# Long-convolution kernels summed in four column tiles instead of two, with half-size staging, an earlier phase product and the first kernel in the scratch tile

## The chip, the cores and the metric

The program runs on one core of one Trainium2 chip. The core has a matrix engine (PE, with its weight loads shown apart as PEld), a vector engine (DVE), an engine for activations and copies (ACT), a general engine (POOL) and an engine that issues transfers (SP); each works through its own list of instructions in order and waits on semaphores for the others. Transfers are carried by sixteen DMA engines; here nearly all are issued by SP and POOL. The metric is the device time of one execution in microseconds (us), given as the median of the runs shown.

## The reference

Four layers on a sequence of 2048 positions with 640 channels: a state-space convolution, attention, the same convolution again, the same attention again, each on a layer norm of x and added to x. The convolution's kernel is computed from the parameters and is the same both times:

```
x = A_u
x = x + _A_ref(_layernorm(x), ...)      # long convolution, kernel K
x = x + _B_ref(_layernorm(x), ...)      # attention, 32 heads of 20, one key and value head
x = x + _A_ref(_layernorm(x), ...)
x = x + _B_ref(_layernorm(x), ...)

# inside _A_ref: D = 640 channels, N = 128 states, L = 2048
dt = exp(log_dt)[:, None];  A = A_re + 1j*A_im;  logdA = dt*A;  dB = dt*Bc
P = exp(logdA[:, :, None] * arange(L))
K = einsum("dn,dnl,dn->dl", Cc, P, dB).real
y = irfft(rfft(u padded to 2L) * rfft(K padded to 2L))[:L] + u * Dskip
```

So K takes 640 x 2048 sums over 128 complex states, before the first convolution can use its spectrum.

## The kernel before

The program has three kinds of stage, one after another: the kernels' generation (`_kgen`), two convolution layers (`conv_layer`, with the kernels' spectra in `kernel_spectra` ahead of the first), and two attention layers.

**Generation.** A position l is split as 32 i + j, with i in 0..63 and j in 0..31. The sum over the states then is a product of two small factors per channel: one of size 128 states x 64 (called `E1R`, for even terms, and `M1`, for odd ones) and one of 128 x 32 (`C2`, `S2`). Channels go in 20 units: unit u takes sixteen pairs of channels ("par" is 0 or 1 within a pair). Sixteen of the units have their pair 128 channels apart and belong to runs of eight that fill two blocks of 128 channels each (q is 0 and 1); the last four fill the fifth block (q is 2). For a unit the code has these steps:

- `phase(u, h)`: PE multiplies a small table into a PSUM tile `ph` (two matmuls of 512 columns), of which there is one; DVE rounds it (`r`) and subtracts (`f`). h is 0 and 1.
- `trig(u, h)`: ACT takes the absolute value (`fa`), a sine and a cosine (`s`, `c`). POOL sets one column of the first pair of tiles ahead of it.
- `sizes(u, k)`, `exps(u, k)`: PE makes exponents in a tile `pe` (two buffers), ACT takes their exponential (`m`), for k of 0, 1, 2.
- `products(u, k)`: DVE multiplies sizes and sines, two operations for each k: `e1r`, then `m`, then `c` and `s`.
- `sums(u, ds)`: PE forms the sums over the states into a tile `pk` (two buffers). For each of 16 values of d and for each of the two terms, two matmuls, one per par, stand in the two halves of the array's columns: 64 columns of weights (`e[u][:, d, par]`) and 32 moving columns (`c[u][:, d, par]`).
- `store(u)`: ACT copies `pk` into a staging tile `kst` for the whole q (one buffer). With the last unit of q, SP writes it to `kd` in DRAM: for q of 0 and 1 with rows of 8 KB, for q of 2 with runs of 256 bytes.

The three engines PE, ACT and DVE keep the order in which the code is written, which is a loop over u in which unit u's phase and sizes, unit u-1's products and unit u-2's sums are interleaved by hand. Within an iteration PE has: `sizes(u, 0)`, sums for d 0 to 2, `sizes(u, 1)`, sums for d 3 to 5, the product of `phase(u + 1, 0)`, sums 6 to 9, the product of `phase(u + 1, 1)`, and the rest (with `sizes(u, 2)` at one of two places as u is odd or even). DVE has: `products(u-1, 0)`, the two operations of `phase(u+1, 0)`, `products(u-1, 1)`, those of `phase(u+1, 1)`, `products(u-1, 2)`, and in iterations 5 to 12 statistics of x. With unit 20 (there is none) the tables are freed and POOL issues the load of the transform's weights `wf`, 4 MB.

**Spectra.** `kernel_spectra` loads the five blocks from `kd` through POOL's queue: four into one tile `kts`, the fifth into a tile `ktl`, which also takes the skip weights. Both lie where tiles of the generation lay. For each block DVE adds the skip weight to position 0 (`skip`, 128 elements), PE multiplies by `wf` (`raw`, four PSUM tiles `zk` of 32 passes each), ACT copies out (`Azk`), DVE forms a transform over eight (`radix`, `fft8`) with two helper tiles `B` and `R`, and SP writes the spectrum. PE and ACT are one block ahead of DVE.

Of the kernel before, what the change touches and what calls it, by code (L numbers as in the profile page):

```python
# [37 lines left out]
SAFE = ((LIMIT - 1e-6) / 1.002) ** 2  # L38

# [103 lines left out]
class Net:  # L143
# [152 lines left out]
    def _kgen(self, ctx):  # L296
# [39 lines left out]
        C1, S1, C2, S2, M1, M2, E1R, F, PE_, PK, KST = ({} for _ in range(11))  # L336
        KST[0] = bp.tile([P, 32, 128], F32, tag="kst", bufs=1, name="kst0")
# [14 lines left out]
        def phase(u, h):  # L352

            pp = kp.tile([P, 1024], F32, tag="ph", bufs=1, name=f"ph{u}{h}")
            src, col, rows = ((tb, 0, 48), (ta, 512, 96))[h]
            for par in range(2):
                nc.tensor.matmul(pp[:, 512 * par : 512 * par + 512], grp(src, u, par, rows),
                                 kg[0:rows, col : col + 512], start=True, stop=True)
            r = bp.tile([P, 1024], BF16, tag="r", bufs=2, name=f"r{u}{h}")
            self.magic_round(r, pp)  # L360
            F[u, h] = bp.tile([P, 1024], F32, tag="f", bufs=4, name=f"f{u}{h}")
            nc.vector.tensor_tensor(F[u, h], pp, r, ALU.subtract)
# [51 lines left out]
        def sums(u, ds):  # L414

            if u not in PK:
                PK[u] = kp.tile([P, 512], F32, tag="pk", bufs=2, name=f"pk{u}")
            for d in ds:
                for e, c, first in ((E1R, C2, True), (M1, S2, False)):
                    for par in range(2):  # L420
                        nc.tensor.matmul(PK[u][64 * par : 64 * par + 64, 32 * d : 32 * d + 32],  # L421
                                         e[u][:, d, par], c[u][:, d, par], start=first, stop=not first)

        def store(u):
            q, r, _, _, run = units[u]
            if r == 0 and q > 0:
                KST[q] = bp.tile([P, 32, run], F32, tag="kst", bufs=1, name=f"kst{q}")
            kst = KST[q]
            nc.scalar.activation(kst[:, :, 16 * r : 16 * r + 16],
                                 PK[u].rearrange("p (d j) -> p j d", d=16), AF.Copy)  # L430
            if 16 * (r + 1) == run:
                for par in range(2):
                    for jh in range(2):
                        src = kst[64 * par : 64 * par + 64, 16 * jh : 16 * jh + 16, :]
                        if run == 128:
                            dst = self.kd[2 * q + par, 64 * jh : 64 * jh + 64]
                            nc.sync.dma_start(dst, src.rearrange("p t d -> p (t d)"))
                        else:
                            dst = self.kd[4, 64 * jh : 64 * jh + 64].rearrange(
                                "p (t d) -> p t d", d=DC)[:, :, 64 * par : 64 * par + 64]  # L440
                            nc.sync.dma_start(dst, src)


# [4 lines left out]
        with tc.manual_schedule(engines=engines):  # L448
            for h in range(2):
                phase(0, h)  # L450
            for u in range(n + 3):
# [18 lines left out]
                if tot:  # L470
                    sums(u - 2, range(3, 6))
# [9 lines left out]
                if tot:  # L481
                    sums(u - 2, range(6, 10))
# [4 lines left out]
                if tot:  # L487
                    sums(u - 2, range(10, 13))
# [8 lines left out]
                if tot:  # L497
                    sums(u - 2, range(13, 16))
# [11 lines left out]
    def conv_setup(self, ctx):  # L510
        tc = self.tc
        if not self.wfs:
            self.conv_weights(self.nc.sync)
        self.cvp = ctx.enter_context(tc.tile_pool(name="cvp", bufs=1, reuse_waits="tile"))

        self.B = self.cvp.tile([P, 16, 256], F32, name="B")
        self.R = self.cvp.tile([P, 8, 256], F32, name="R")
# [166 lines left out]

    def kernel_spectra(self):

        nc, cv = self.nc, self.cvp

        kts = cv.tile([P, 4, 16, DC], F32, tag="wi", name="kts")
        ktl = cv.tile([P, 24, DC], F32, tag="xn", name="ktl")  # L690
        ks = [kts[:, c] for c in range(4)] + [ktl[:, 0:16]]
        dsk = ktl[0:1, 16:21]
        nc.gpsimd.dma_start(dsk.rearrange("p c d -> p (c d)"), self.ins["A_Dskip"][None, :])
        for c in range(NCH):
            nc.gpsimd.dma_start(ks[c].rearrange("p t d -> p (t d)"), self.kd[c])

        def skip(c):
            k = ks[c][0:1, 0]
            nc.vector.tensor_tensor(k, k, dsk[:, c], ALU.add)

        skip(0)
        Z = {0: self.raw(ks[0], "k0")}
        for c in range(NCH):
            if c + 1 < NCH:
                skip(c + 1)
                Z[c + 1] = self.raw(ks[c + 1], f"k{c + 1}")
            A = cv.tile([P, 16, 256], F32, tag="kh", bufs=2, name=f"kn{c}")
            weave(self.radix(Z.pop(c), A) + fft8(nc, A, self.B, self.R, -1), ())
            nc.sync.dma_start(self.kh[c], A.rearrange("p s d -> p (s d)"))

    def conv_layer(self, nm, first):
# [4 lines left out]
        B, R = self.B, self.R  # L716
        tt = nc.vector.tensor_tensor
        with tc.manual_schedule(engines={mybir.EngineType.PE, mybir.EngineType.Activation,
# [7 lines left out]
            if first:  # L726
                self.kernel_spectra()

# [604 lines left out]
```

## Time and profile before

| what | us |
|---|---|
| median of 3 runs (3068.69 to 3069.82) | 3069.56 |
| the profiled execution | 3071.17 |
| its span, from the first to the last instruction | 3069.4 |
| from the span's start to the first copy of sums into `kst` | 85.3 |
| from there to the last such copy | 252.7 |
| first matmul of the spectra | 344.1 |

The profile is of one execution. Its views name an instruction by engine, line of the code, operation and `out<-in`; "x4" after it is how many were put together in a row. In a timeline the columns are the start, the time that the row took, the engine, the line and the operation, and in square brackets how long the engine had stood idle before and what ended that. In a list of waits the numbers are the total, how often, and the longest. A single-precision matmul stands in the trace as two passes. Ends of matmuls are modelled, so the distance between starts says more than the duration. The line numbers are those of the kernel before; after the change they are higher.

### The profile page before, as it was taken

What the parts mean: (1) busy time and instruction counts of PE and PEld (TensorE: products, weight loads), DVE (VectorE), ACT (ScalarE), POOL (GpSimd) and SP (SyncE); (2) the same over time, 40 slices, a digit from 0 to 9 for tenths busy, and PEclk for the clock granted to TensorE, in tenths of its full rate; (3) what the DMA queues carried; (4) which work ended last, traced back from release to release, by engine and by line L of the source; (5) the groups of instructions that cost most, each with busy time, mean ns of one, the idle gap of its engine ahead of it and who ended that gap; (6) DMA issues with size and microseconds to landing.
All of it is one profiled execution on the core that took longest, in us unless ns stands there. A gap on an engine that the chain in (4) does not pass through costs nothing. (4 is left out here: it accounts for less than half of the span.)

```text
span 3069.4 us, 52317 instructions
## 1 busy us (share of the span) xinstructions
PE 2874.8 (94%) x21696; PEld 1362.8 (44%) x21696; DVE 1404.4 (46%) x1793; ACT 2428.3 (79%) x2910; POOL 41.5 (1%) x113
## 2 busy tenths in 40 slices
PE   2888898989899999999999989798999999999999
PEld 0555887867323323333233479673223333333233
DVE  7888799972122232232222399922122222222223
ACT  5777343353899999999999633446999999999997
POOL 0000000000100000000000000000000000000000
PEclk9999999989999999999999999899999999999999
DMA  6010551123300010000100210132000100100100
GB/s 143 18 29 17 177 220 56 38 83 131 112 24 25 22 28 22 24 25 22 27 23 24 112 55 28 50 125 79 23 22 25 39 27 24 39 25 21 45 19 22
DMA packets 72177, 158.82 MB, mean 52 GB/s; under 512 B 21509, under 2 KB 27653, under 8 KB 67797
## 3 DMA queue, kind: packets, MB, share of 16 engines
q1 hardware_dynamic: 65880, 137.70, 14.9%
q0 software_dynamic: 4080, 16.67, 1.5%
q8 instruction: 175, 2.87, 0.4%
q10 hardware_dynamic: 1968, 0.98, 0.1%
q14 instruction: 74, 0.60, 0.1%
HBM read 95.22 MB, written 48.04 MB: 47 GB/s over the span
## 5 line engine op out<-in xcount | busy, mean ns | idle before, releaser
L1134 ACT ACTIVATE pt<-scb 128x1024 f32<-128x1024 f32 x1024 | 942.2, 1115 | 7.5 <-PE scb L1130 5.8
L1134 ACT ACTIVATE pt<-scd 128x1024 f32<-128x1024 f32 x1024 | 942.2, 1118 | 7.0 <-PE scd L1130 5.5
L1144 PE MATMUL pod<-pt,vt 128*32 128x512 f32 x4096 | 546.9, 606 | 4.4 <-DVE on L1161 0.8
L1144 PE MATMUL pob<-pt,vt 128*32 128x512 f32 x4096 | 546.9, 606 | 4.3
L1130 PE MATMUL scb<-qpb,kt 62*128 62x512 f32 x2048 | 386.0, 451 | 6.2 <-PEq L1079 5.8
L1130 PE MATMUL scd<-qpd,kt 62*128 62x512 f32 x2048 | 385.8, 451 | 5.8 <-PEq L1079 5.5
L1130 PEld LDWEIGHTS scd<-qpd,kt 62*128 62x128 f32 x2048 | 166.1, 185 | 402.0 <-ACT pt L1134 392.3
L1130 PEld LDWEIGHTS scb<-qpb,kt 62*128 62x128 f32 x2048 | 165.9, 185 | 402.1 <-ACT pt L1134 392.6
L1192 DVE TENSOR_TENSOR x<-pyd,x 128x320 f32<-128x320 f32 x146 | 71.7, 491 | 561.0 <-PE pyd L1204 561.0
L1192 DVE TENSOR_TENSOR x<-pyb,x 128x320 f32<-128x320 f32 x146 | 71.7, 491 | 547.7 <-PE pyb L1204 547.7
L1164 DVE RECIPROCAL rc<-rc 128x512 f32<-128x512 f32 x62 | 207.9, 3353 | 2.1
L1144 PEld LDWEIGHTS pob<-pt,vt 128*32 128x32 f32 x4096 | 80.7, 108 | 178.3 <-issue 160.3
L1144 PEld LDWEIGHTS pod<-pt,vt 128*32 128x32 f32 x4096 | 80.6, 108 | 177.7 <-issue 159.7
L421 PE MATMUL pk<-s,m 128*64 128x32 f32 x1280 | 130.8, 295 | 13.3 <-DVE s L412 13.3
L421 PE MATMUL pk<-c,e1r 128*64 128x32 f32 x1280 | 132.1, 297 | 11.4 <-DVE c L411 11.2
L421 PEld LDWEIGHTS pk<-c,e1r 128*64 128x64 f32 x1280 | 105.3, 221 | 79.6 <-issue 52.2
L579 PE MATMUL za<-xna,wf 128*128 128x256 f32 x512 | 113.0, 383 | 2.7 <-ACT xna L733 2.7
L421 PEld LDWEIGHTS pk<-s,m 128*64 128x64 f32 x1280 | 108.1, 226 | 15.9 <-DVE s L412 15.9
L579 PE MATMUL zc<-xnc,wf 128*128 128x256 f32 x512 | 111.5, 379 | 2.7 <-ACT xnc L733 2.7
L581 ACT ACTIVATE Aa<-za 128x1024 f32<-128x1024 f32 x16 | 16.4, 1023 | 118.3 <-PE za L579 116.9
L581 ACT ACTIVATE Ac<-zc 128x1024 f32<-128x1024 f32 x16 | 16.4, 1024 | 113.7 <-PE zc L579 113.7
L579 PEld LDWEIGHTS za<-xna,wf 128*128 128x128 f32 x512 | 98.0, 192 | 16.7 <-ACT xna L733 3.3
(308 smaller groups left out, 3272.9 us busy)
## 6 DMA issues: line engine op xcount, KB each, us to landing
kh<-kh SPq DMA_DIRECT2D x10, 2048.0 KB
kh<-kn SPq DMA_DIRECT2D x5, 2048.0 KB
qhd<-qh SPq DMA_DIRECT2D x40, 256.0 KB
qld<-ql SPq DMA_DIRECT2D x40, 256.0 KB
qpb<-qhd SPq DMA_DIRECT2D x256, 40.0 KB
qpd<-qhd SPq DMA_DIRECT2D x256, 40.0 KB
ot<-on SPq DMA_DIRECT2D x216, 40.0 KB
wf<-in_c_wf POOLq DMA_DIRECT2D x16, 512.0 KB, 7.9
```

Source lines behind the costliest of these rows:

```text
L421: nc.tensor.matmul(PK[u][64 * par : 64 * par + 64, 32 * d : 32 * d + 32], e[u][:, d, par], c[u][:, d, par], start=first, stop=not first)
L579: nc.tensor.matmul(zv[:, :, c, kk], self.wf[:, t + 4 * h, j, c, kk], x, start=(n == 0), stop=(n == 3))
L581: nc.scalar.activation(A.rearrange("p (o s) d -> p o s d", o=2)[:, :, 2 * t : 2 * t + 2], z.rearrange("p (c o e) -> p o c e", c=2, o=2), A ...
L1130: nc.tensor.matmul(sc[:, 512 * par : 512 * par + 512], kt[rows, 128 * t : 128 * t + 128], qps[nb, hg, pr][rows], start=True, stop=True)
L1134: nc.scalar.activation(pt, sc, AF.Exp, scale=SCALE)
L1144: nc.tensor.matmul(po[32 * j : 32 * j + 32], vt[:, t], pts[step, j // 2][:, 512 * (j % 2) : 512 * (j % 2) + 512], start=(t == 0), stop=(t ...
L1164: nc.vector.reciprocal(rc, rc)
L1192: nc.vector.tensor_tensor(xh, py, xh, ALU.add)
```

## The change

Five edits go together.

- **Four column tiles.** `sums` exchanges the operands: the weights are now the factor of 32 columns, the moving operand that of 64, and four matmuls (two par, and channels d and d + 8) stand in the four quarters of the array's columns. A unit has 64 matmuls as before. `sums` counts d to 8 instead of 16, and the interleaving is cut anew. The channels of the inputs are permuted ahead of the launch so that the results come out in order.
- **Half staging tiles.** `kst` holds four units instead of eight, in two buffers. It is laid out with 128 partitions of (quarter, j) and 64 x 32 elements, and is written after each four units in eight transfers, whose rows in DRAM are runs of 32 elements, 128 bytes.
- **The skip weights** no longer are added by DVE. POOL issues a transfer that accumulates onto `kd` in DRAM (for the fifth block onto the loaded tile): two while unit 10's sums are stored, two at the end of the generation, one after the last load.
- **The next phase's product first.** `phase` is split: `phase_first(u + 1, 0)` issues its two matmuls right behind `sizes(u, 0)`, ahead of all sums of that iteration. DVE's part stays where it was.
- **The first kernel in the scratch tile.** `R` is allocated when it is needed, and block 0 is loaded into a first version of it; blocks 1 to 3 go to `kts`, block 4 to `ktl`.

```
+        def phase_first(u, h):
+            pp = PH[u, h] = kp.tile([P, 1024], F32, tag="ph", bufs=1, name=f"ph{u}{h}")
+            ... the two matmuls ...
         def phase(u, h):
+            if (u, h) not in PH:
+                phase_first(u, h)
+            pp = PH.pop((u, h))
...
             for d in ds:
                 for e, c, first in ((E1R, C2, True), (M1, S2, False)):
-                    for par in range(2):
-                        nc.tensor.matmul(PK[u][64 * par : 64 * par + 64, 32 * d : 32 * d + 32],
-                                         e[u][:, d, par], c[u][:, d, par], start=first, stop=not first)
+                    for s in range(4):
+                        dd, par = 8 * (s % 2) + d, s // 2
+                        nc.tensor.matmul(PK[u][32 * s : 32 * s + 32, 64 * d : 64 * d + 64],
+                                         c[u][:, dd, par], e[u][:, dd, par], start=first, stop=not first)
...
+            h, g = divmod(r, 4)
+            if g == 0 and u > 0:
+                KST[q, h] = bp.tile([P, 64, 32], F32, tag="kst", bufs=2, name=f"kst{q}{h}")
...
+            if g == 3:
+                for s in range(4):
...
                     for jh in range(2):
+                        dst = kd[64 * jh : 64 * jh + 64].rearrange("i (t d) -> t i d", d=DC)[:, :, c0 : c0 + 32]
+                        nc.sync.dma_start(dst, kst[32 * s + 16 * jh : 32 * s + 16 * jh + 16])
+            if r == 2 and q > 0:
+                for c in (2 * q - 2, 2 * q - 1):
+                    self.skip(c, self.kd[c, 0:1, 0:DC])
...
                     sizes(u, 0)
                     if odd:
                         exps(u, 0)
+                if nxt:
+                    phase_first(u + 1, 0)
                 if tot:
-                    sums(u - 2, range(0, 3))
+                    sums(u - 2, range(0, 2))
...
+    def skip(self, c, k):
+        self.nc.gpsimd.dma_start(k, self.ins["A_Dskip"][None, c * DC : (c + 1) * DC], accum_op=ALU.add)
...
+        ks = [self.scratch("k0").rearrange("p a b -> p (a b)").rearrange("p (t d) -> p t d", t=16)]
         kts = cv.tile([P, 4, 16, DC], F32, tag="wi", name="kts")
         ktl = cv.tile([P, 24, DC], F32, tag="xn", name="ktl")
-        ks = [kts[:, c] for c in range(4)] + [ktl[:, 0:16]]
+        ks += [kts[:, c] for c in range(3)] + [ktl[:, 0:16]]
...
+            if c == 0:
+                self.R = self.scratch("k")
```

On PE, in an iteration in the middle of the generation (`tm` and `tb` are tables, `pe` the exponents, `ph` the phase product, `pk` the sums of unit 2), there stood before:

```order
L385 MATMUL pe_636<-kg,tm 128x512
L421 MATMUL pk_639<-c_2_446,e1r_510 64x32 x2
L421 MATMUL pk_639<-s_2_447,m_2_489 64x32 x2
...
L385 MATMUL pe_652<-kg,tm 128x512
...
L357 LDWEIGHTS tb
L357 MATMUL ph_667<-kg,tb 128x512
```

and now:

```order
L404 MATMUL pe_636<-kg,tm 128x512
L371 LDWEIGHTS tb
L371 MATMUL ph_639<-kg,tb 128x512
...
L441 MATMUL pk_642<-e1r_510,c_2_446 32x64 x4
L441 MATMUL pk_642<-m_2_493,s_2_447 32x64 x4
...
L404 MATMUL pe_659<-kg,tm 128x512
```

The phase product `ph` has moved from behind twelve rows of sums and a second `pe` to right behind the first `pe`; each row of sums is four matmuls of 32 x 64 where it was two of 64 x 32.

On POOL, at the end of the generation (`kd` is the kernels in DRAM), there stood before:

```order
L368 MEMSET s_19_2437 128x32
L532 DMA wf<-in_c_wf 128x1024 x8
L693 DMA ktl<-in_A_Dskip 1x16x40
L695 DMA kts<-kd 128x2048 x4
L695 DMA ktl<-kd 128x2048
```

and now:

```order
L387 MEMSET s_19_2465 128x32
L554 DMA wf<-in_c_wf 128x1024 x8
L709 DMA kd<-in_A_Dskip 16x8 x2
L720 DMA Rk_2750<-kd 128x2048
L720 DMA kts<-kd 128x2048 x3
L720 DMA ktl<-kd 128x2048
L709 DMA ktl<-in_A_Dskip 1x16x8
```

The load of the first block goes to `R` ahead of the others, with the skip weights of blocks 2 and 3 ahead of it, and it no longer stands behind a transfer into `ktl`.

More of the change, by code (lines that the diff above doesn't have):

```diff
@@ L38, with channel_order @@
 SAFE = ((LIMIT - 1e-6) / 1.002) ** 2
+def channel_order():
+    order = []
+    for start, run in ((0, 128), (128, 128), (256, 128), (384, 128), (512, 64), (576, 64)):
+        for r in range(run // 16):
+            for dh in range(2):
+                c = start + run // 2 * dh + 8 * r
+                order += range(c, c + 8)
+    return np.array(order)
+CHANNELS = channel_order()
 def host_constants():
```

54 lines of the change are left out of this document (22 added, 32 removed).

## The prediction

> **What bounds the kernel now.** I first read the busy slices and then went to the generation alone, as nothing else is changed; the two attention layers and the second convolution keep their instructions. The busy time by pairs of units (from one copy into the staging tile to the next but one) says what limits the steady part; columns are the span, then busy time of PE, weight loads, DVE, ACT and POOL.
>
> ```profile
> core 0: us, PE busy (x) PEld busy (x) DVE busy (x) ACT busy (x) POOL busy (x), PEclk, DMA share, GB/s
> 85.27:113.61 28.34, 25.20 (x277) 15.84 (x277) 23.23 (x21) 21.79 (x22) 0.63 (x4) 1.00 0.00 1
> 141.94:170.21 28.27, 25.23 (x277) 15.84 (x277) 25.14 (x27) 21.80 (x22) 0.62 (x4) 1.00 0.01 1
> 283.55:311.88 28.34, 25.25 (x277) 15.84 (x277) 23.22 (x21) 21.79 (x22) 0.63 (x4) 1.00 0.34 75
> ```
>
> A pair takes 28.3 us whether DVE has 23.2 us of work in it or, with the statistics, 25.1. So DVE isn't the limit, and neither is ACT at 21.8: a loop through several engines is. The list of waits from 0 to 420 us (first row), that from 85.3 to 312 us (the others) and a piece of the timeline give the loop:
>
> ```profile
> DVE r L177 <- PE ph L357: 41.8, 20, 5.9
> ...
> DVE r L177 <- PE ph L357: 31.0, 16, 2.5
> ACT m L395 <- PE pe L385: 26.1, 16, 2.3
> ACT m L393 <- PE pe L385: 21.5, 15, 2.4
> ```
>
> ```profile
> 154.55 1.22 DVE L362 TENSOR_TENSOR f<-ph,r 128x1024 f32<-128x1024 f32 x1
> 155.70 1.21 DVE L411 TENSOR_TENSOR c<-c,m 128x1024 f32<-128x1024 f32 x1
> 156.83 1.22 DVE L412 TENSOR_TENSOR s<-s,m 128x1024 f32<-128x1024 f32 x1
> 158.10 0.43 PE L421 MATMUL pk<-s,m 128*64 128x32 f32 x4 [0.71 <-DVE s L412]
> 158.34 0.41 PE L421 MATMUL pk<-c,e1r 128*64 128x32 f32 x4
> 159.32 1.03 PE L385 MATMUL pe<-kg,tm 48*128 48x512 bf16 x2
> 160.13 1.22 DVE L404 TENSOR_TENSOR e1r<-m,c 128x1024 f32<-128x1024 f32 x1
> 160.28 0.43 PE L421 MATMUL pk<-c,e1r 128*64 128x32 f32 x4
> 161.70 1.03 PE L357 MATMUL ph<-kg,tb 48*128 48x512 bf16 x2
> 162.77 1.22 DVE L177 TENSOR_SCALAR r<-ph 128x1024 bf16<-128x1024 f32 x1 [1.43 <-PE ph L357]
> ```
>
> DVE finishes `s`; only then can PE start the sums; behind them and a `pe` stands the next phase product; and on that DVE waits, once per unit, 31.0 us in sixteen units. The single `ph` tile is already free at the end of `f` (154.55 + 1.22 = 155.77), six us before PE gets to it.
>
> The end of the generation and the first spectrum, on all engines:
>
> ```profile
> 317.58 1.03 PE L385 MATMUL pe<-kg,tm 96*128 96x512 bf16 x2
> 318.93 4.37 POOL L532 DMA_DIRECT2D wf<-in_c_wf  x8 [9.46 <-PE pe L385]
> 331.12 0.43 PE L421 MATMUL pk<-s,m 128*64 128x32 f32 x4 [0.62 <-DVE s L412]
> 337.54 0.41 PE L421 MATMUL pk<-s,m 128*64 128x32 f32 x4
> 337.99 0.60 ACT L429 ACTIVATE kst<-pk 128x512 f32<-128x512 f32 x1 [7.49 <-PE pk L421]
> 338.63 2.11 POOL L695 DMA_DIRECT2D kts<-kd  x4
> 344.12 21.05 PE L550 MATMUL zk<-kts,wf 128*128 128x128 f32 x162 [6.18 <-DMA kts<-kd]
> 350.75 1.02 ACT L552 ACTIVATE Azk<-zk 128x1024 f32<-128x1024 f32 x1 [10.63 <-PE zk L550]
> 354.26 1.02 ACT L552 ACTIVATE Azk<-zk 128x1024 f32<-128x1024 f32 x1 [2.49 <-PE zk L550]
> 362.47 1.29 DVE L560 TENSOR_TENSOR kn<-Azk 128x512 f32<-128x512 f32 x2 [2.28 <-ACT Azk L552]
> 374.50 0.27 DVE L699 TENSOR_TENSOR kts<-kts,ktl 1x128 f32<-1x128 f32 x1
> 374.70 4.89 DVE L560 TENSOR_TENSOR kn<-Azk 128x512 f32<-128x512 f32 x8
> 404.09 1.95 PE L550 MATMUL zk<-ktl,wf 128*128 128x128 f32 x16
> ```
>
> The path runs through PE's last sums, a load of 5.5 us (338.63 to 344.12) on which PE waits, four quarters of the first block, and from 362.47 on through DVE without a gap. What moves DVE's row at 362.47 moves the rest of the program with it.
>
> **The change, part by part.**
>
> *The sums.* A row of four passes takes 0.214 us where they follow each other: 30 rows from 331.12 to 337.54, 6.42 us. So two tiles' weights, 128 columns in all, and 32 moving columns go by in 0.107 us, twice per row. Now four tiles of 32 weight columns, again 128 in all, and 64 moving ones make a round. Attention has four column tiles at once:
>
> ```profile
> 901.39 1.07 PE L1144 MATMUL pob<-pt,vt 128*32 128x512 f32 x8
> 902.39 0.74 PE L1130 MATMUL scb<-qpb,kt 62*128 62x512 f32 x4
> 438.88 28.96 PE L579 MATMUL za<-xna,wf 128*128 128x256 f32 x126 [0.46 <-ACT xna L733]
> ```
>
> Eight passes of 512 columns in 1.00 us there are two rounds of four tiles, 0.98 ns per column, so 64 columns need 0.063 us: under 0.107. The transform loads 128 weight columns per pass at 21.05 / 162 = 0.13 us, start included. I take 0.107 us per round, 32 rounds, 3.4 us per unit for 6.8. The lower bound is 0.063 (2.0 us), the upper that each of the 128 passes keeps its present 0.0535 us (6.8).
>
> *The early product.* It goes to where PE waits for nothing but `f`: at about 155.8 in the piece above, done by 157.0, while DVE still has `c`, `s` and two `e1r` to do, until 161.35. So `r` follows without a gap, with 4 us to spare. Behind it on PE stand the sums, which couldn't have started before `s` (156.83 + 1.22) anyway. PE's work per unit falls to 3.4 + 5 x 0.96 for the `pe` and `ph` = 8.2 us (one takes from 159.32 to 160.28), against 11.6 of DVE. What is late next is ACT, with 21.8 of what becomes 23.2 per pair; its own waits for `pe` are 47.6 us in that list and shrink, as fewer sums stand ahead of `pe`. The term lies between 0 and 31.0; I take 30.0, close to the whole, since all three engines keep room. Ahead of 85.3 us one such wait has a like place (nearest row: the 2.5 us of the list); 2.4, between 0 and 10.8 (41.8 less 31.0; most of it is for tables).
>
> *The end.* The last sums have nothing to wait for after `s`: half of 331.12 to 337.75, 3.3 us. In the iteration before, `pe` at 317.58 stands behind twelve rows of sums, of which half the time goes: 12 x 0.107 = 1.3, with the order's cut 1.7. Together 5.0, between 1 and 6.6.
>
> *The first load.* Before, it waited for the very last sums, as its queue's first entry went into their tiles. Now `R` lies over the tiles of unit 18's sines and unit 19's `f`, which are long done; it waits for the first weight loads, and its bytes stand behind theirs:
>
> ```profile
> 322.00:324.00 2.00, 2.00 (x42) 2.00 (x42) 0.00 (x0) 2.00 (x2) 1.30 (x3) 1.00 1.01 395
> 330.00:332.00 2.00, 1.31 (x22) 1.21 (x22) 1.97 (x4) 0.50 (x1) 0.00 (x0) 1.00 0.71 281
> ```
>
> 4 MB at some 400 GB/s from 318.93 are in by 331.5, 12.6 us; 1 MB more is 2.6 us and landing 1: 16.2 us after the weights' issue, which comes 1.35 after the start of `pe`. From that `pe` to the last sums' end it is 337.75 - 317.58 = 20.2 before and 16.9 after (3.3 shorter). So the block lands at 17.6, 0.7 us after PE is ready; before, PE stood 6.4 us. I take 5.0; bounds 0 and 6.4.
>
> *Skip weights.* DVE's path loses three additions between 374 and 407, 0.20 each (374.50 to 374.70): 0.6. POOL's accumulating transfers carry 512 bytes; the two at unit 10 wait for writes issued three units earlier, and behind them on POOL stands only a column to be set, needed a unit later. No cost, at most a us or two.
>
> *The staging.* ACT copies the same 512 elements per partition (0.60 at 337.99). The writes become 8192 runs of 128 bytes per four units, where the last block had 4096 runs of 256. All transfers of SP's queue between 336 and 362 us were these and a few more:
>
> ```profile
> q1 hardware_dynamic: 4160, 1.05, 20.1%
> ```
>
> 20.1% of 16 engines for 26 us by 4160 is 20 ns a run, so 8192 take 10 us if a short run costs as much; nobody waits for them for three units. Only the last four units' writes have a reader, the load of block 4: they start with the end of the sums, share the engines with three blocks' loads (8 us), are in after some 20 us, and the block after 26, with its skip weight at 29. PE asks for it after four blocks, 344.12 to 404.09 before: 60 us. Cost nothing; 30 us to spare.
> The Trainium skill ("DMA: Bandwidth & Descriptors", Specifications) gives 512 bytes as the least for full rate and says that below it the engine reads, modifies and writes. If that doubled the 20 ns, the writes would be 10 us longer, inside the 30 to spare, so the sum stays; no run here yet shows a 128-byte run.
>
> The sum: 30.0 + 2.4 + 5.0 + 5.0 + 0.6 = 43.0. Against the profiled execution's 3071.17 this gives 3028.2; the runs' median is 1.6 lower, and I forecast 3026.5 us.
>
> **The rivals.**
>
> *PE starts the first block at full rate* (0.15). 11 matmuls stand in the two us from 346, 21 in those from 356, and the first quarter took 6.63 us (344.12 to 350.75) for 3.5 of the next:
>
> ```profile
> 346.00:348.00 2.00, 2.00 (x11) 2.00 (x11) 0.28 (x1) 0.00 (x0) 0.00 (x0) 1.00 1.04 424
> 356.00:358.00 2.00, 2.00 (x21) 2.00 (x20) 0.61 (x2) 0.16 (x1) 0.53 (x1) 1.00 0.00 0
> ```
>
> If that comes of the 6.2 us without work ahead of it, it goes with them, and another 3.1: 3023.5. Against it: the granted clock stands at 1.00 in both rows, and I can't see that PE ran at full rate before the gap. The Trainium skill ("TensorE: Matmul & The Clock Gate", Part 1) says that PE falls to half clock after an idle window of about 3.4 us and comes back after one of work; the gap and the halved rate agree with it.
>
> *The passes' issue is the limit, not the weights* (0.15): 6.8 us of sums per unit remain. PE then has 2 x 11.6 and some 2 us of waits per pair, 25.3 for 28.3: 8 pairs give 23 for 30, the end 1 for 5: 3069.6 - 32 = 3037.6.
>
> *ACT takes the wait over* (0.07): half of the 30 stays, 3041.5. For it speaks that 21.8 of 23.2 us leave 6%, against it that no wait of DVE on ACT is in the list.
>
> *The early product isn't early* (0.03): if `f` came late, PE would stand at the product with the sums queued behind; 30.0 and 2.4 fall away, 3059. The 4 us to spare speak against it. Nearer to nothing, 0.01.
>
> *Four tiles run one after another* (0.06), the other side: a pass of 64 columns then costs a round, 0.107, and a unit 13.7 + 4.8 = 18.5 us for 14.17: 4.3 x 18 more in the steady part, 7 at the end, less 5.6 of the load and skip: 3148. It decides from sums of 9.4 us per unit, 0.073 per pass, on. Attention's row is against it: eight passes of 512 one by one, at the transform's 28.96 / 126 per 256, would be 3.7 us, not 1.00.
>
> *The short writes hold up block 4* (0.03): slower than before from 10 + 30 + 43 = 83 us for the last 8192 on, 160 ns a run: over 3070.
>
> The forecast itself has 0.50, with 3019 to 3032 as its own range. The range of 3018 to 3043 leaves out the last three. A measurement of this kernel tells about 0.2% (6 us) from no change: faster 0.90, same 0.02, slower 0.08.
>
> **What would show it.** Pairs of 23 to 25.5 us with DVE busy throughout, and no wait of `r` on `ph`; 0.21 us for eight passes of the sums; about 7 us less between the start of the last `pe` and the first `zk`; DVE's first long run of `kn` starting near 319. Wrong it would be if DVE's idle time came back under another name (ACT's `c` or PE's `ph`), if the sums' passes kept 0.053 us, or if PE waited for `R` or for block 4.

## The result, and the profile after

The changed kernel takes 3025.8 us (3024.5 to 3027.3) where the kernel before takes 3069.7 in runs beside it: a ratio of 0.9856, with a 95% interval of 0.9844 to 0.9867. The profiled execution took 3025.52 us, 45.65 less than the one before. The landmarks of the sum, from the two traces:

| stretch | before, us | after, us | gain | predicted |
|---|---|---|---|---|
| start to the first copy of sums into `kst` | 85.3 | 83.1 | 2.2 | 2.4 |
| sixteen units | 226.6 | 196.3 | 30.3 | 30.0 |
| from there to the last copy | 26.1 | 20.1 | 6.0 | 5.0 |
| last copy to the first `zk` | 6.1 | 1.1 | 5.0 | 5.0 |
| first `zk` to DVE's fourth quarter of block 0 | 18.3 | 17.2 | 1.1 | 0 |
| behind that | | | 1.1 | 0.6 |
| sum | | | 45.7 | 43.0 |

In one of the experiments below, the first with extra matmuls, the profiled execution ran at a granted clock of 0.65 in the mean and took 3891 us; nothing is read from its trace.

Busy time by pairs of units after the change, one pair without the statistics of x and two with (span, then PE, weight loads, DVE, ACT and POOL, each with its number of rows, then the granted clock, DMA share and GB/s):

```profile
83.08:107.45 24.37, 18.13 (x278) 8.26 (x277) 24.16 (x22) 21.70 (x24) 0.62 (x4) 1.00 0.01 1
131.81:156.17 24.36, 17.20 (x278) 8.17 (x277) 24.09 (x27) 21.68 (x23) 0.62 (x4) 0.57 0.04 6
205.38:230.69 25.31, 18.42 (x278) 8.22 (x277) 25.07 (x25) 21.68 (x23) 1.41 (x5) 0.50 0.29 36
```

A pair takes 24.4 us for 28.3. DVE is busy in all of it, as forecast. But the busy time says more than the share: before, such a pair held 23.23 us of DVE's work in 21 operations, and the first row here holds 24.16 in 22. DVE does more than a pair's work per pair; it is running ahead. Its `c` products show how fast it goes when nothing but its own work is in the way:

```profile
82.02 1.22 DVE L430 TENSOR_TENSOR c<-c,m 128x1024 f32<-128x1024 f32 x1
93.61 1.22 DVE L430 TENSOR_TENSOR c<-c,m 128x1024 f32<-128x1024 f32 x1
...
276.30 1.22 DVE L430 TENSOR_TENSOR c<-c,m 128x1024 f32<-128x1024 f32 x1
```

That is 11.59 us per unit between the first two, 23.2 per pair, and 194.3 us for sixteen units with eight statistics in them, against 196.3 for ACT's copies. So something other than DVE sets 24.36 in the pairs without statistics. The list of waits (the first row from 0 to 400 us, the others from 83 to 280) names it:

```profile
DVE r L191 <- PE ph L371: 7.9, 3, 5.5
...
PE ph L371 <- DVE f L381: 28.9, 20, 2.8
ACT m L412 <- PE pe L404: 15.8, 8, 2.8
PE pe L404 <- ACT m L412: 13.7, 7, 3.7
ACT m L414 <- PE pe L404: 5.4, 16, 0.5
```

The wait of `r` on `ph` (41.8 us over this stretch before) is down to three, all ahead of the first copy. In its place ACT waits for `pe` 15.8 + 5.4 = 21.2 us, 2.65 per pair: 21.7 of work and 2.65 of waiting are the 24.36. The timeline of PE and ACT shows why:

```profile
155.73 1.03 PE L404 MATMUL pe<-kg,tm 48*128 48x512 bf16 x2
156.56 1.06 PE L371 MATMUL ph<-kg,tb 48*128 48x512 bf16 x2
157.55 0.44 PE L441 MATMUL pk<-e1r,c 128*32 128x64 f32 x8
...
158.56 1.03 PE L404 MATMUL pe<-kg,tm 48*128 48x512 bf16 x2
159.63 1.02 ACT L412 ACTIVATE m<-pe 128x1024 f32<-128x1024 f32 x1 [1.80 <-PE pe L404]
```

The early product and four rows of sums, the first of them shown, stand ahead of the second `pe`, and ACT waits 1.80 us for that.

The end of the generation and the first block, from all engines:

```profile
283.84 4.23 POOL L554 DMA_DIRECT2D wf<-in_c_wf  x8 [9.64 <-PE pe L404]
292.27 0.57 POOL L720 DMA_DIRECT2D Rk<-kd  x1 [1.99 <-ACT c L396]
...
296.04 0.44 PE L441 MATMUL pk<-m,s 128*32 128x64 f32 x8 [0.60 <-DVE s L431]
...
299.02 0.44 PE L441 MATMUL pk<-m,s 128*32 128x64 f32 x8
299.53 0.60 ACT L450 ACTIVATE kst<-pk 128x512 f32<-128x512 f32 x1 [6.50 <-PE pk L441]
300.63 16.12 PE L572 MATMUL zk<-Rk,wf 128*128 128x128 f32 x128 [1.17 <-DMA Rk<-kd]
306.13 1.02 ACT L574 ACTIVATE Azk<-zk 128x1024 f32<-128x1024 f32 x1 [1.69 <-PE zk L572]
...
317.85 1.29 DVE L582 TENSOR_TENSOR kn<-Azk 128x512 f32<-128x512 f32 x2 [2.28 <-ACT Azk L574]
```

From 296.04 to 299.02 it is fourteen steps from one row of eight passes to the next, 0.213 us each, as forecast. The first `zk` waits 1.17 us for block 0, whose bytes follow the weights', and the first quarter took 5.50 us (300.63 to 306.13) for 3.5 of the next. The granted clock, the third number from the end in the rows by windows, changes within that quarter:

```profile
300.60:303.90 3.30, 3.27 (x15) 3.30 (x16) 3.16 (x11) 0.83 (x1) 0.00 (x0) 0.50 0.99 390
304.00:307.30 3.30, 3.30 (x31) 3.30 (x31) 1.62 (x10) 1.24 (x2) 0.00 (x0) 1.00 1.05 345
```

PE has 15 passes in 3.3 us at 0.50 and 31 at 1.00; "half rate" and "full rate" below mean these two. DVE's long run starts at 317.85, where 319 was forecast.

### The profile page after: what moved, and what is told of

It reads as the page before. It is cut to its first block, busy times and chain, and to the rows that moved or that the text cites. A ratio compares the mean times of both kernels' runs of the same rounds, so it can differ in the third digit from the quotient of the medians.

```text
span 3023.7 us, 52365 instructions
## 1 busy us (share of the span) xinstructions
PE 2797.2 (93%) x21696; PEld 1284.0 (42%) x21696; DVE 1402.3 (46%) x1788; ACT 2427.3 (80%) x2910; POOL 45.1 (1%) x117
## 3 DMA queue, kind: packets, MB, share of 16 engines
q1 hardware_dynamic: 102680, 137.70, 15.7%
## 5 line engine op out<-in xcount | busy, mean ns | idle before, releaser
L1228 PE MATMUL pyd<-wo,ot 128*32 128x320 f32 x1168 | 105.3, 432 | 0.0
L1228 PE MATMUL pyb<-wo,ot 128*32 128x320 f32 x1168 | 105.3, 432 | 0.0
L601 PEld LDWEIGHTS zc<-xnc,wf 128*128 128x128 f32 x512 | 96.9, 190 | 16.3 <-ACT xnc L757 3.3
L800 PE MATMUL yc<-Ac,wi 128*128 128x128 f32 x640 | 78.4, 286 | 15.8 <-DVE Ac L114 13.1
```

The lines of the kernel that those rows point to most:

```text
L601: nc.tensor.matmul(zv[:, :, c, kk], self.wf[:, t + 4 * h, j, c, kk], x, start=(n == 0), stop=(n == 3))
L800: nc.tensor.matmul(y[:, s * DC : (s + 1) * DC], self.wi[:, t, j, c_, kk], v[:, 2 * t + c_, kk], start=(i == 0 and not whole), stop=(i == 3 ...
L1228: nc.tensor.matmul(py[j : j + m], o[:, 128 * i + j : 128 * i + j + m], w[:, 320 * half : 320 * half + 320], start=start, stop=stop)
```

## The experiments

The kernel before took 3069.0 to 3070.5 us beside them. Differences of one or two us between experiments are read from landmarks in the traces, each of one execution, since the medians can't tell them.

### 1. The order alone

In the kernel before, the phase product is split off and put ahead of the sums; all else stays.

```
+                if nxt:
+                    phase_first(u + 1, 0)
                 if tot:
                     sums(u - 2, range(0, 3))
```

> The kernel before with one edit: the next phase product stands ahead of all sums of its iteration; sums in two column tiles, staging and loads as before. Theory (order and sums each give a part): the wait of DVE's r on ph goes, but PE keeps 6.8 us of sums and 4.8 of products per unit, 11.6 against DVE's 11.6 (12.7 with statistics), with small waits of its own; pairs of about 25.3 us for 28.3, so 23 to 24 of the 30 us in the sixteen units, 2 ahead of them, nothing at the end and at the load: about 3044 us. Rival A (the order alone gives the whole steady gain, the sums count only at the end): pairs of 24.4, 32 us less, 3037 us. Rival B (PE's sums are the bound, the order only moves the wait): over 3060 us, with a wait of ACT or DVE on PE in the place of the old one.

Measured: 3051.2 us (3049.9 to 3052.8), ratio 0.9942 (0.9928 to 0.9956), so 18 us, not 25. The sixteen units take 212.2 us, 14.4 less. A pair by windows, and one line of the waits over the sixteen units:

```profile
109.62:136.08 26.46, 24.51 (x277) 16.09 (x277) 23.72 (x23) 21.80 (x23) 0.62 (x4) 1.00 0.01 2
```

```profile
DVE r L177 <- PE ph L357: 13.4, 8, 2.5
PE pe L390 <- ACT m L398: 14.3, 8, 2.0
```

PE has 24.5 us of work in 26.5 and waits for ACT in 1.8 of the other 2: with 6.8 us of sums per unit PE and its wait for ACT are the limit, and `r` still waits once per pair. The theory was right in kind and 1.2 us per pair too good.

### 2. Four tiles alone

The changed kernel without the early product; the staging, the skip weights and the new order of the sums stay.

```
-                if nxt:
-                    phase_first(u + 1, 0)
```

> The changed kernel with the early product taken back: the phase product stands again behind the first sums and the second exponents. Theory: ahead of the product now stand sums of three d in rows of 0.213 us, two rows each, 1.28 us, where there were twelve rows of 0.214, 2.57; of the old wait of 1.94 us per unit 1.29 goes and 0.65 stays, 10 us in the sixteen units and about 1 ahead of them; the end and the load as in the changed kernel: about 3037 us. Rival A (the order is all that counts in the steady part): the 30 us come back, 3056 us. Rival B (four tiles alone free PE enough): within 2 us of the changed kernel, 3026 to 3028 us.

Measured: 3037.1 us (3036.2 to 3037.7), ratio 0.9897 (0.9882 to 0.9912), the theory's 3037. A pair, and the wait that is left:

```profile
109.82:135.66 25.84, 18.63 (x278) 8.06 (x276) 24.23 (x24) 21.69 (x24) 0.63 (x4) 1.00 0.29 37
```

```profile
DVE r L191 <- PE ph L371: 10.9, 16, 1.2
```

10.9 / 16 = 0.68 us per unit, 0.65 expected. Over the sixteen units the tiles alone give 19.1 us (226.6 to 207.5), the order alone 14.4, both 30.3: neither edit has the steady gain by itself.

### 3. Block 0 in `kts` instead of the scratch tile

```
-        ks = [self.scratch("k0")...]
-        ks += [kts[:, c] for c in range(3)] + [ktl[:, 0:16]]
+        ks = [kts[:, c] for c in range(4)] + [ktl[:, 0:16]]
```

> The changed kernel, but block 0 is loaded into kts with blocks 1 to 3, and not into a version of R. Theory (the head of the queue decides): the load was late before because the first entry of POOL's queue went into the tiles of the very last sums; kts itself lies over tiles that are done by about 291.5 us in the changed kernel's time, so the load starts at 292 as with R, lands at 299.5 to 300.5, and nothing changes: 3025 to 3027 us. Rival, by the prediction's wording (the scratch tile brings the 5 us): PE stands again some 5 us for the first block, 3030 to 3032 us.

Measured: 3024.0 us (3023.8 to 3024.8), ratio 0.9855 (0.984 to 0.987): not slower. The load and its reader:

```profile
291.83 0.57 POOL L719 DMA_DIRECT2D kts<-kd  x1 [2.03 <-ACT c L396]
300.10 5.14 PE L572 MATMUL zk<-kts,wf 128*128 128x128 f32 x43 [1.12 <-DMA kts<-kd]
```

The issue is as early as with `R` within half a us, and the wait is the same 1.1 us. The scratch tile isn't what brought the load forward.

### 4. The skip weights' transfers alone

The kernel before, with the skip weights accumulated in DRAM as in the change, so that no transfer into `ktl` heads POOL's queue and DVE no longer adds them.

```
-        nc.gpsimd.dma_start(dsk..., self.ins["A_Dskip"][None, :])
...
+            if r == 2 and q > 0:
+                for c in (2 * q - 2, 2 * q - 1):
+                    self.skip(c, self.kd[c, 0:1, 0:DC])
```

> The kernel before with one edit: the skip weights are added by accumulating transfers as in the change, so that the transfer into ktl no longer heads POOL's queue; block 0 stays in kts, order, sums and staging as before. Theory (the head of that queue made the first load late): kts is free when m of unit 19 is formed, some 9 us ahead of the last sums' end, the load is issued at about 329 instead of 338.6 and its bytes land with the weights' by 335.5; the first zk follows the last sums, 6 us sooner, and the first block loses its slow start in part; DVE saves 0.6: 3061 to 3064 us against 3070. Rival (the load also needs R, as the prediction had it): PE still waits 5 us or more for the first block, 3068 to 3070 us.

Measured: 3062.3 us (3061.1 to 3063.8), ratio 0.9975 (0.9966 to 0.9984): 7.8 us by this edit alone. POOL in the kernel before, where the transfer at the head waits for the last sums, then POOL and PE here:

```profile
338.04 0.51 POOL L693 DMA_DIRECT2D ktl<-in_A_Dskip  x1 [14.74 <-PE pk L421]
```

```profile
329.77 2.08 POOL L700 DMA_DIRECT2D kts<-kd  x4 [6.26 <-DVE m L409]
337.90 0.41 PE L421 MATMUL pk<-s,m 128*64 128x32 f32 x4
338.24 1.01 PE L553 MATMUL zk<-kts,wf 128*128 128x128 f32 x3
```

The load is issued nine us earlier (338.63 before) and PE goes on without a gap; from the first `zk` to DVE's fourth quarter it is 16.7 us for 18.3. By the landmarks 6.2 us come at the load and 1.6 in the first block. With experiment 3 this settles the load: the queue's head held it.

### 5. ACT's loop: the second exponents first

The changed kernel; in odd iterations the exponents for k = 1 stand ahead of the product and the sums.

```
+                if now and odd:
+                    sizes(u, 1)
+                    exps(u, 1)
                 if nxt:
                     phase_first(u + 1, 0)
```

> The changed kernel, but in odd iterations the exponents for k = 1 stand ahead of the next phase product and of the first sums. Theory A (ACT's loop is the limit after the change): ACT's pairs are 24.36 us, constant, 21.7 of work and 2.5 of waits for pe that stands behind the product and four rows of sums, while DVE without statistics needs 23.3 per pair and draws ahead of ACT by some 2 us up to the end; with the wait gone pairs without statistics fall to 23.3, and the end of the generation comes 2 to 3 us sooner: 3022 to 3024 us, ACT's wait for pe at its second exponential (15.8 us in the sixteen units) below 5. Theory B (DVE is the limit, as it shows no gap in these units): the waits of ACT fall, the time does not, 3025 to 3026.5 us.

Measured: 3023.2 us (3021.0 to 3023.8), ratio 0.985 (0.9837 to 0.9863). A pair, and ACT's longest wait:

```profile
106.59:130.68 24.09, 16.55 (x278) 7.86 (x277) 23.85 (x23) 21.58 (x24) 0.62 (x4) 0.70 0.29 36
```

```profile
ACT m L414 <- PE pe L404: 21.7, 17, 2.8
```

The total is theory A's, but not by its way. The wait at the second exponential is gone and has come back at the third, and pairs fall by 0.27 us only, not to 23.3. Of the 2.6 us against the changed kernel, 1.5 lie in the first block's rate by the traces (below). This didn't tell A from B.

### 6. One product less on DVE

The changed kernel without DVE's product of S2 with M2, so that the sums' odd terms lack a factor.

```
-                tt(S2[u], S2[u], M2[u], ALU.mult)
```

> The changed kernel without DVE's product of S2 with M2 (one of ten operations per unit, 1.13 us; the sums' odd terms then lack a factor). Theory A (in pairs without statistics the loop of ACT and PE, 24.36 us, is the limit, DVE only with statistics): pairs stay at 24.36, the sixteen units take 194.9 for 196.3, and at the end DVE's saved operation and its lead bring another 1 to 2 us: 3022 to 3024 us. Theory B (DVE is the limit throughout): 1.13 us per unit, 18 us in the steady part and 2 more around it: 3006 us.

Measured: 3022.5 us (3021.7 to 3023.9), ratio 0.9845 (0.983 to 0.986). The first pair:

```profile
82.73:107.10 24.37, 17.86 (x278) 8.26 (x277) 20.95 (x19) 21.70 (x23) 0.62 (x4) 1.00 0.06 19
```

Eighteen us of DVE's work were taken out of sixteen units, and the pairs without statistics did not move by 0.01 us; the sixteen units went from 196.3 to 194.9, as theory A had it. In these pairs the loop of ACT and PE is the limit.

### 7. All three exponents first, statistics last

The changed kernel with block 0 loaded ahead of the weights (experiment 9), all three exponents ahead of the product in odd iterations, and the eight statistics of iterations 5 to 12 moved behind the last products.

```
+                if now and odd:
+                    sizes(u, 1)
+                    exps(u, 1)
+                    sizes(u, 2)
+                    exps(u, 2)
                 if nxt:
                     phase_first(u + 1, 0)
...
-                if 5 <= u < 13:
-                    self.stats(u - 5)
-                for t in {n: range(8, 12), n + 1: range(12, 16)}.get(u, ()):
+                for t in {n: range(0, 4), n + 1: range(4, 16)}.get(u, ()):
```

> The changed kernel with block 0 loaded ahead of the weights, in odd iterations all three exponents ahead of the next phase product and of the sums, and the eight statistics of x that DVE forms in iterations 5 to 12 put behind the last products. Theory (after the change the loop of ACT and PE is the limit in pairs without statistics, DVE in those with): both go, pairs fall to DVE's twice 11.63, 23.3 us, all eight of them; the sixteen units take 186 to 187 for 196.3; behind the last s DVE now has sixteen statistics of 1.0 us and the norm ahead of the first block's fourth quarter, so of the 10 us some 2 to 3 are given back there: 3016 to 3019 us. Rival (the loop of ACT stays, as in the experiment in which only the second exponents were moved, 24.1 per pair): 193 us for the sixteen units, and the statistics cost at the end what they saved: 3021 to 3024 us.

Measured: 3013.9 us (3011.9 to 3014.7), ratio 0.9814 (0.98 to 0.9827). This beats both kernels, by 12 us the changed one. A pair, and two lines of the waits from 278 to 315 us:

```profile
104.83:128.08 23.25, 16.32 (x277) 7.98 (x276) 23.04 (x21) 21.48 (x23) 0.62 (x4) 0.57 0.32 39
```

```profile
ACT sq L679 <- DVE ve L697: 11.8, 1, 11.8
PE zk L571 <- ACT Azk L573: 2.9, 1, 2.9
```

All pairs are at DVE's 23.25, the sixteen units at 186.0. At the end some is given back: ACT's root of the norm stands ahead of the first block's copies and waits 11.8 us for DVE's statistics, so that from the first `zk` to the fourth quarter it is 21.5 us. Moving that root behind the copies wasn't tried.

### 8. A product on POOL

As 7, with the statistics where they were, and the product of S2 with M2 on POOL.

```
-                tt(S2[u], S2[u], M2[u], ALU.mult)
+                nc.gpsimd.tensor_tensor(S2[u], S2[u], M2[u], ALU.mult)
```

> The changed kernel with block 0 ahead of the weights and the three exponents first in odd iterations (statistics where they were), and the product of S2 with M2 on POOL instead of DVE. Theory (POOL is free and takes up to 4 us for it without disturbing DVE): DVE has 10.5 us per unit, 11.6 with statistics, ACT 21.7 per pair becomes the limit; pairs of 22 to 23.2 us, sixteen units 178 to 184 for 196.3, in all 3007 to 3014 us. Rival (POOL's product holds up DVE's operations beside it, or comes too late for the sums): DVE's operations grow beyond 1.22 us or PE waits for s, pairs of 24 us or more, 3022 us and up.

Measured: 3029.6 us (3028.3 to 3034.1), ratio 0.9864 (0.9849 to 0.9879), in the rival's range, but only in part by its mechanism. DVE's `c` product by the groups of lines (busy us, mean ns), and POOL and DVE in the timeline:

```profile
L430 DVE TENSOR_TENSOR c<-c,m 128x1024 f32<-128x1024 f32 x16 | 35.9, 2243 | 0.0
```

```profile
130.05 2.35 POOL L431 TENSOR_TENSOR s<-s,m 128x1024 f32<-128x1024 f32 x1 [1.78 <-ACT m L414]
130.37 3.11 DVE L430 TENSOR_TENSOR c<-c,m 128x1024 f32<-128x1024 f32 x1
```

DVE's `c` beside POOL's product takes 2.24 us in the mean for 1.22 alone, so most of the 1.22 that DVE saves it loses. In the rows shown it ends 1.1 us after POOL's product, about its own length. Beside the next product (POOL from 141.12 to 143.66) DVE had `r` and `f`, which read `ph` in PSUM, and they kept 1.22 us each. The Trainium skill ("GPSIMD Engine Reference", Specifications) says that POOL's way into SBUF is shared with DVE and that they contend where a DVE instruction has two SBUF inputs. The rows agree.

The time against the changed kernel is lost elsewhere. The sixteen units take 192.5 us, 3.8 less than in the changed kernel, and DVE's fourth quarter comes 1.8 us sooner (316.02). Then DVE stands until the last staging writes are out:

```profile
323.78 2.36 DVE L114 TENSOR_TENSOR B<-kn 128x1024 f32<-128x1024 f32 x2 [6.47 <-DMA kd<-kst]
```

In the changed kernel this row follows its quarter without a wait. What the product on POOL would bring without this wait was not measured; the profiled execution was also the slowest of the four (3034.1 us).

### 9. Block 0 ahead of the weights

```
         for c in range(NCH):
+            if c == 1:
+                self.load_weights(self.wf, "c_wf", nc.gpsimd)
             nc.gpsimd.dma_start(ks[c]...)
```

> The changed kernel, but POOL issues the load of block 0 into R ahead of the eight loads of the transform's weights, not behind them. Theory (the first block's bytes are what PE waits for after the change, 1.2 us; R is free by 281 us): they land before 290, the first zk follows the last sums within 0.3 us, 1.1 us sooner, and as PE then goes on without a gap the slow first sixteen passes shrink too, up to 1.5 us: 3023 to 3025 us. Rival A (the first half of the weights lands later by the block's 2.6 us and becomes the wait): nothing gained, 3025 to 3027 us. Rival B (what PE waits for isn't this load): the gap of 1.2 us stays.

Measured: 3023.9 us (3021.9 to 3024.7), ratio 0.9848 (0.9835 to 0.9862). POOL and PE:

```profile
280.63 0.76 POOL L710 DMA_DIRECT2D kd<-in_A_Dskip  x1 [4.52 <-DMA kd<-kst]
...
299.23 2.03 PE L573 MATMUL zk<-Rk,wf 128*128 128x128 f32 x9
302.43 0.82 PE L573 MATMUL zk<-Rk,wf 128*128 128x128 f32 x5 [1.17 <-issue]
```

The load of block 0 follows the row at 280.63 at once. The wait for the block is gone, but after the first passes PE stands 1.17 us for nothing that the profile shows. DVE's fourth quarter comes 0.8 us sooner (317.07).

### 10 and 11. Extra matmuls in PE's idle time

Twenty-two on the changed kernel, with eight more behind the last sums; then sixteen on the kernel of experiment 9. Their result isn't used.

```
+                if u == n + 1:
+                    keep_busy(16)      # nc.tensor.matmul(warm, ident, ident) each
                 if u >= 3:
                     store(u - 3)
```

> The changed kernel with 22 extra matmuls (128 x 128, single precision, their result is not used) on PE in the 6.7 us in which it waits for the last c, and 8 more behind the last sums. Theory (PE halves its rate after a stretch without work and takes some 3 us of dense work to come back): the last unit's rows of eight passes take 0.11 us for 0.213, the sums end 1.7 us sooner, the first sixteen passes of the first block take 1.8 us for 3.3; the block's data still land at 300.5, so the first zk starts where it did: 1.5 us less in all, 3024 us. Rival (the half rate comes of the weights' transfers that run at 400 GB/s beside it, not of the idle time): rows stay at 0.213, nothing changes, or the extra matmuls cost up to 2 us, 3026 to 3028 us.

> The changed kernel with block 0 loaded ahead of the weights and 16 extra matmuls (128 x 128, single precision, result not used) on PE in the 6.5 us in which it waits for the last c. Theory (PE halves its rate after a stretch without work): the last unit's rows of eight passes take 0.11 us for 0.213, the sums end 1.7 us sooner, the first block follows at 297.6 at full rate, sixteen passes in 1.8 us: against the kernel with only the block ahead (3023.9 us) 1.7 us plus up to 1.5: 3020.5 to 3022.5 us. Rival (the half rate comes of the weights' transfers beside it): rows stay at 0.213 us and the time within 1 us of 3023.9.

The first took 3024.5 to 3027.6 us in its other four executions, no different from the changed kernel. The second took 3023.6 us (3022.4 to 3026.8), ratio 0.9848 (0.9834 to 0.9861), as without the extra work; but its trace tells more. PE:

```profile
295.62 0.32 PE L441 MATMUL pk<-m,s 128*32 128x64 f32 x8 [0.34 <-DVE s L431]
296.87 0.29 PE L441 MATMUL pk<-e1r,c 128*32 128x64 f32 x8
...
300.12 0.26 PE L441 MATMUL pk<-m,s 128*32 128x64 f32 x4 [2.92 <-issue]
300.59 1.60 PE L583 MATMUL zk<-Rk,wf 128*128 128x128 f32 x12
```

Eleven steps from row to row between 295.62 and 296.87, 0.114 us each for 0.213, with the loads still coming in beside them at some 400 GB/s, so the transfers don't set the rate. The granted clock stands at 1.00 from 295.1 us on here, behind 4.2 us of extra matmuls, and in the changed kernel at 0.50 from 290.3 to 304.0. The first block's first sixteen passes take 1.9 us for 3.45. But PE then stood 2.92 us with no releaser in the profile, and the 1.7 us were gone. What held it is open; in both cases of such a stop the list of DMA queues has one packet of an instruction queue in it or just ahead of it, beside DMA engines that are 95 to 100% busy with the loads, which fits late instructions but doesn't show it.

### 12. Every write twice

```
+                        for _ in range(2):
                             nc.sync.dma_start(dst, kst[...])
```

> The changed kernel with every write of the staging tiles to DRAM issued twice: 16384 runs of 128 bytes per four units for 8192. Theory (writes are off the path, 30 us to spare at block 4): no change, 3025 to 3027 us; the last four units' writes are in 10 us later, block 4's load 10 us later, and PE still has it in time. Rival (short writes cost more than 20 ns a run, or their bytes hold up the blocks' loads): PE waits for block 4 or for the first block, over 3030 us.

Measured: 3047.1 us (3046.6 to 3049.1), ratio 0.9924 (0.9908 to 0.9939): 21 us slower than the changed kernel, in the rival's range. The queues of the staging writes from 115 to 150 us, of the changed kernel and of this one (packets, MB, share of 16 engines):

```profile
q1 hardware_dynamic: 8320, 1.05, 23.5%
```

```profile
q1 hardware_dynamic: 16640, 2.10, 49.2%
```

POOL, PE and DVE at the end of the generation, with every write twice:

```profile
304.85 0.77 POOL L710 DMA_DIRECT2D kd<-in_A_Dskip  x1 [13.57 <-DMA kd<-kst]
305.48 0.72 POOL L721 DMA_DIRECT2D Rk<-kd  x1
...
314.27 3.97 PE L573 MATMUL zk<-Rk,wf 128*128 128x128 f32 x17 [15.02 <-DMA Rk<-kd]
...
341.85 3.56 DVE L114 TENSOR_TENSOR B<-kn 128x1024 f32<-128x1024 f32 x4 [7.71 <-DMA kd<-kst]
```

A run of 128 bytes costs 0.235 x 35 x 16 / 8320 = 15.8 ns, no more than the 20 of a run of 256 before (those had the blocks' loads beside them). But the writes have readers that wait. Those of units 12 to 15 are waited for at once: the skip weights' transfer at the head of POOL's queue needs them, and block 0's load stands behind it. Those of the last four units hold up DVE's first `B`. Of the 23.6 us between the two traces some 14 lie at the first `zk` and 7.7 at `B`.

## Why the prediction was right, point by point

That 3026.5 us were forecast and 3025.8 measured is closer than the terms deserve: by the landmarks the change gained 2.7 us more than the sum, and the profiled execution before was 1.5 us above the median beside it.

- **The steady stretch** (30.0; measured 30.3). The mechanism is shown by taking it apart: product late, 0.68 us of waiting per unit stay (experiment 2); sums long, PE and its wait for ACT fill the pair (experiment 1). "What is late next is ACT" was right, and more than a shadow: the prediction expected DVE's 23.2 us to rule the pairs, and in pairs without statistics ACT's loop of 24.36 does (experiment 6). It cost little, since DVE ran ahead and spent its lead where the statistics stood: 196.3 us against DVE's own 194.3. The rival "ACT takes the wait over" was thus true in kind, for 2 us and not 15.
- **The sums' rate** (0.107 us per round of four passes; measured 0.213 per eight). The passes and the moving columns doubled at no cost, and the 128 weight columns per round stayed, so these fit as what sets the rate. The lower bound of 0.063 us wasn't one: it was taken from attention, where the granted clock is 1.00, and where the rows of sums run at full rate a round takes 0.056 (286.9 to 288.0 in the changed kernel). The price of the rival with unchanged passes was too low: 25.3 us per pair, where experiment 1 measured 26.46, so by an estimate that case would have gained 14.4 and some 9 us around it and ended near 3046, outside the range.
- **Ahead of 85.3 us** (2.4; 2.2), **the skip weights and what lies behind** (0.6; 1.1): right in the main.
- **The end** (5.0; 6.0). The last sums from 331.12 to 337.75 before and from 296.04 to 299.24 now are 3.4 us shorter, as forecast; the other 2.6, put at 1.7, was under-sized.
- **The first load** (5.0; 5.0). The size and the arithmetic of the bytes were right: the block landed 1.2 us after PE was ready, 0.7 forecast. The step that gave the credit to `R` is not borne out. The prediction said both that the queue's head was the obstacle and that `R` lies over tiles long done; experiments 3 and 4 leave the first alone. Whether `R`'s place was long free isn't shown either: by the row at 292.27 its load stood 1.99 us for ACT's last `c`, as the load into `kts` did in experiment 3, while in experiment 9 it goes out at 281.3, ahead of that `c`.
- **The first block** (0; 1.1). The prediction gave the full rate 3.1 us and a chance of 0.15. It came in part here, and by 2.6 to 2.7 us in experiments 2, 3, 5 and 6 (15.6 to 15.7 us from the first `zk` to the fourth quarter for 18.3). "The granted clock stands at 1.00 in both rows", which spoke against it, was misread: the trace of the kernel before has its first clock record at 349.80 us, and ahead of it the column shows 1.00 whatever PE does. PE was at half rate before the gap too: a `pe` took 0.96 us there, as it does at 0.50 in the changed kernel (158.56 to 159.52). At 349.8 the passes' distance goes from 0.21 to 0.11 us, 5.7 us behind the first `zk`; in the changed kernel a record of 1.00 stands 3.3 us behind it (303.97); in the four experiments it stands 1.3 to 1.9 us ahead of it. Half of the time at half rate is lost: 2.4 us less of it here make 1.2, 5.7 less make 2.9. The Trainium skill ("TensorE: Matmul & The Clock Gate", Part 1) has PE return to full clock after some 3.4 us of work counted in a window that runs freely. A start that is fast in one trace and slow in the next by the same program text but for a tile's place (experiment 3) agrees with that, and so does the record of 0.50 ahead of it, from 290.32 to 303.97, four times 3.41 us. So how much of this term came was luck, and the sum didn't carry it.
- **The staging at no cost** held, but "30 us to spare" at block 4 left out two nearer readers. Experiment 9 shows the skip weights' transfer waiting for units 12 to 15's writes until 280.63; in the changed kernel it is issued at 288.2, behind the weights: some 7.6 us of room. And DVE's first `B` waits for the last units' writes, 7.71 us in experiment 12, 6.47 in 8, 0.7 in 2 and 0.5 in 3. In the changed kernel it starts at 319.06 without a wait, and the last packets of these writes start at 317.9. So the room was about a us, and that nothing was paid there was luck.

## What to carry to other kernels

Look at what stands ahead of a product in its engine's order as well as at how long that work takes: here the earlier product alone gave 14.4 us and the shorter sums alone 19.1, both together 30.3, and only together did the wait go. A busy share near one doesn't name the limit: count the operations in the stretch against what the stretch needs, and take work out of the suspected engine. Ask of each DMA queue what its first entry waits for; taking one small transfer from the head brought 7.8 us. And ask what lies over a tile that is still being written out: doubled staging writes cost 21 us, at the queue's head and at a tile of DVE.

## What the runs showed that was not expected

- **A granted clock of 1.00 can mean that nothing is recorded yet.** In the kernel before, the column shows 1.00 from 0 to 30 us, where PE has no matmul, and in the generation, where rows of sums take 0.21 us; its first clock record is at 349.80. In experiments 1 and 2 it is the same up to 329.9 and 297.5, in the changed kernel up to 116.2. From the first record on, the column and the rate agree: in all traces with four tiles that are read here, rows of eight passes are 0.21 us apart at 0.50 and 0.11 at 1.00. Ahead of it they are 0.21 apart, and only the distance between rows tells the rate.
- **PE can stop without a releaser.** Where PE's work moved ahead while the weights and blocks came in, it stood 1.17 us (experiment 9) and 2.92 us (experiment 11) on "issue", and took back most of what the move had brought.
- **DVE and POOL get in each other's way** where both operands of DVE's are in SBUF: `c` went from 1.22 us to 2.24 in the mean, and to 3.11 beside a product of 2.35 us on POOL, while `r` and `f`, reading PSUM, kept 1.22.
